# A cubic and a power of two as two bf16 tiles from GpSimd, multiplied on VectorE, in a fused SSM and attention kernel

## The chip, the cores and the metric

The kernel runs on one core of one Trainium2 chip. The metric is the device time of one execution in microseconds; the time before is the median of three runs.

## The reference

One input `x` of 2048 rows and 1024 columns (bf16) goes through two branches, and a gate mixes them row by row:

```python
g = sigmoid((x * gate_w).sum(-1, keepdims=True))
# branch A: a diagonal complex state space model, 1024 states
Lam_bar = exp(dt * Lam);  B_bar = ((Lam_bar - 1.0) / Lam)[:, None] * Bmat
Bu = einsum("bld,pd->blp", x, B_bar)
h  = Lam_bar * h + Bu[:, t]              # for t in 0 .. 2047
a  = 2.0 * einsum("blp,dp->bld", hseq, Cmat).real + x * Dskip
# branch B: attention, 32 heads of 32 columns
q, k, v = split(x @ wqkv);  p = softmax(q k^T * 32 ** -0.5);  b = (p v) @ wo
out = g * a + (1 - g) * b
```

## The kernel before

The kernel records operations in an order that it plans by itself, engine by engine, and each engine then runs its list in order, waiting on semaphores where an operation needs another engine's result.

**Bursts.** Attention is cut into 8 groups of four heads, each into 8 units of 256 queries, each into 8 bursts of 256 keys: 512 bursts, and the loop variable `p` of `build` counts them (64 to a group; `pg` is the place in the group). `burst` (L1612) issues the scores on TensorE (L1624, eight matmuls into four banks) and two exps on ScalarE (L1643), each over 1024 columns: `exp(0)`, and later `exp(1)`. `pv` (L1709) multiplies earlier exps with V into bank 6. At the end of a unit `normalize` (L1722, L1723, then a transposing DMA) takes the result out. The score banks form three slots, so the scores of the next burst wait for `exp(0)` of this one.

**Dense work.** The other matmuls run in the gaps, four of 512 columns to a burst, all in bank 7, in chains of eight to twenty: B's product `u` (L1457), projections of Q, K and V for the next group (L1426, L1445), C's product `c` (L1504), and at the end the output projection (L1535). VectorE evacuates bank 7 after each chain (L1461, L1433, L1451, L1517, L1547). VectorE also does the scan of the state space model in `item_ops` (L1353, L1362), from u tiles that go out to memory and come back (`ld_u`, L1474).

**VectorE's exps.** ScalarE is relieved of part of the exps. For bursts that are chosen by `X_PLAN` and `X_AT`, `exp(1)` takes only 768 columns (L1640), and VectorE computes the exp of the last 256. Two such bursts make a pair. `x_in` (L1633) scales the scores to a fixed-point number of 32 bits, whose upper half is the integer part and whose lower half is the fraction of a power of two. `x_ops` then takes three f32 steps on VectorE over the 512 columns of the pair: two steps of a cubic in the fraction (L1667, L1668), and a third that adds the integer part (L1664); GpSimd scales that sum into 16 bits that are read as a bf16 (L1665). `x_pv` (L1688) multiplies them with V, at a fixed burst (`x_when`). `exp(1)` waits for `x_in`.

**The plan of VectorE.** In every burst the planner fills the time until the next evacuation with ready work: first the pair's steps (`xbg`), then scan items (`bg`), then the rest (`bg2`), by costs that are written in the code (0.73 for the steps of a pair, `X_LAST` for the last). `dve_t` is the time at which the plan has VectorE free.

**Weights.** All loads are issued by SP's queue in order. Q's weights have one buffer and are loaded at `pg` 28 for the next group; those of K and V have two buffers and are loaded at `pg` 25, a group earlier. C is loaded (L1081) two tiles in every fourth burst from `C_LOADS` = 28 on. The rows of Wo are loaded into buffers that have come free: two rows at burst 386, four when the last chain of C is done, one shortly after the last projections, and one row into B's place.

Of the kernel before, what the change touches and what calls it, by code (L numbers as in the profile page):

```python
# [6 lines left out]
BF = mybir.dt.bfloat16  # L7
# [3 lines left out]
ALU = mybir.AluOpType  # L11
# [720 lines left out]
class GpPhaseA:  # L732
# [24 lines left out]
    def first(self, name):  # L757
        return self.alias.pop(name, [])
# [164 lines left out]
GROUPS = 8  # L923
# [6 lines left out]
REST = 508  # L930
FIRST = 16
RING = 60
C_LOADS = 28

X_AT = ((0, 2), (4, 6), (0, 4))
X_PLAN = (64, 72, 80, 88, 92, 96, 100, 104, 108, 112, 116, 120, 124, 128, 132, 136, 144, 152, 160, 168, 172, 176, 180, 184, 188, 192, 200, 208, 216, 224, 228, 232, 236, 240, 244, 248, 252, 256, 260, 264, 272, 280, 288, 296, 304, 312, 316, 320, 324, 328, 332, 336, 344, 352, 356, 360, 364, 368, 372, 376, 380, 384, 388, 392, 396, 400, 404, 408, 412, 416, 420, 424, 428, 432, 436, 440, 444, 448, 452, 456, 460, 464, 468, 472, 476, 480, 484, 488, 492, 496, 500, 504)
# [12 lines left out]
class Dense:  # L949
# [9 lines left out]
class FastPath:  # L959

    def __init__(self, nc, S, es, d, flag):
        self.nc, self.S, self.d, self.flag = nc, S, d, flag
        E = es.enter_context
        T = lambda name, shape, dt: E(nc.sbuf_tensor("f_" + name, shape, dt))
# [9 lines left out]
        self.wq = wb[:, 0:1024].rearrange("p (a n) -> p a n", a=8)  # L974
        self.wkv = wb[:, 1024:5120].rearrange("p (s q a n) -> p s q a n", s=2, q=2, a=8)
        self.bT = wb[:, 5120:8192].rearrange("p (s a n) -> p s a n", s=3, a=8)

        row = lambda o, n: wb[:, o:o + 1024 * n].rearrange("p (a n) -> p a n", a=n)
        self.wo3 = [row(1024, 2), row(5120, 3), row(3072, 1), self.cT[0][:, 0:1, :], self.cT[0][:, 1:2, :]]
        self.wo = [(self.wo3[0][:, a, :], "wo0") for a in range(2)] + [(self.wo3[4][:, 0, :], "wo4")] + [(self.wo3[1][:, a, :], "wo1") for a in range(3)]  # L980
        self.wo += [(self.wo3[3][:, 0, :], "wo3"), (self.wo3[2][:, 0, :], "wo2")]
# [5 lines left out]
        self.hpx = wb[:, 5120:8192].rearrange("p (k n) -> p k n", k=6)  # L987
        ub = T("ub", [128, 2, 2, 512], BF)
        self.ub = [ub[:, 0], ub[:, 1]]
        self.tq = T("tq", [128, 2, 512], BF)  # L990
        self.xi = T("xi", [128, 2, 2 * X_COLS], I32)
        self.xq = T("xq", [128, 2 * X_COLS], F32)
        self.xp = T("xp", [128, 2 * X_COLS], BF)
        self.ut = T("ut", [128, 2, 512], F32)
        self.ht = T("ht", [128, 2, 512], BF)
        self.prow = self.ht[0:40, 0, 0:128]
# [66 lines left out]
                     [], [("xr", r + k) for k in range(n // 128)], "ld_x", eng)  # L1063

    def w_of(self, g, part):
        return (self.wkv[:, g % 2, part - 1], ("w", g % 2, part)) if part else (self.wq, ("w", 0, 0))

    def ld_w(self, g, part, eng="sp"):
        cb = 1024 * part + 128 * g
# [583 lines left out]
    def x_ops(self, b):  # L1653

        xi, xq, xp = self.xi[:, b % 2], self.xq, self.xp
        lo = xi.bitcast(mybir.dt.uint16)[:, 0::2]
        hi = xi.bitcast(mybir.dt.int16)[:, 1::2]
        bits = xp.bitcast(mybir.dt.int16)[:]
        w = 65536.0
        i2, p2 = [("xi", b % 2, 0), ("xi", b % 2, 1)], [("xp", 0), ("xp", 1)]  # L1660

        def last():
            assert self.x_out == len(self.x_done)
            self.dve(lambda e: e.scalar_tensor_tensor(xq[:], hi, 128.0 / X_K, xq[:], ALU.mult, ALU.add), i2 + ["xq"], ["xq"], "x_q")  # L1664
            self.pool(lambda e: e.tensor_scalar(bits, xq[:], X_K, 128.0 * (E0 + 126.0), ALU.mult, ALU.add), ["xq"], p2, "x_p")  # L1665
            self.x_done.add(b)
        return [(0.73, 0.0, lambda: self.dve(lambda e: e.scalar_tensor_tensor(xq[:], lo, E2 / E3 * w, lo, ALU.add, ALU.mult), i2, ["xq"], "x_q")),  # L1667
                (0.73, 0.0, lambda: self.dve(lambda e: e.scalar_tensor_tensor(xq[:], xq[:], E1 / E3 * w * w, lo, ALU.add, ALU.mult), ["xq"] + i2, ["xq"], "x_q")),  # L1668
                (X_LAST, 0.0, last)]

    def x_flush(self):
        c, wait, f = self.xbg.pop(0)
        f()
        self.dve_t += c

    def x_pv(self, b):

# [56 lines left out]
    def build(self):  # L1734
# [7 lines left out]
        self.begin()  # L1742
        for m in range(3):
            self.ld_b(m)
        for part in (1, 2):
            self.ld_w(1, part)
        self.plan()
        self.pt_own = {}
        self.x_of, self.x_batch, self.x_when = {}, [], {}
        self.xbg, self.x_done, self.x_out = [], set(), 0  # L1750
        self.opening()

        S.tok_w["O"] = S.tok_w[("bank", 6)]
# [25 lines left out]
        outs, k = [], 0  # L1779
# [2 lines left out]
            k += kind != "rest"  # L1782
        cur = None
        first = FIRST
        wo1 = wo6 = last = False
        nal = nc = 0
        self.c_end = 0
        log = self.log = []
# [1 line left out]
        for p in range(first, NBURST):  # L1790
# [38 lines left out]
            while self.later and self.later[0][0] <= p:  # L1829
                self.later.pop(0)[1]()  # L1830

            if pg == 25 and g + 2 < GROUPS:
                assert g or not (proj[0] or cur and cur.tag == "proj")
                for part in (1, 2):
                    self.ld_w(g + 2, part)
            if pg == 28 and g + 1 < GROUPS:
                assert not (cur and cur.tag == "proj")
                self.ld_w(g + 1, 0)
            wsv = self.d["B_wo"].rearrange("(a p) n -> p a n", p=128)
            if p == 386:  # L1840
                self.dma(lambda e: e.dma_start(self.wo3[0], wsv[:, 0:2, :]), [], ["wo0"] + [("w", 0, q) for q in (1, 2)], "ld_wo")
            if not cs and cur is None and not wo1 and self.c_left[3] == 0:
                wo1 = True
                self.dma(lambda e: e.dma_start(self.wo3[1], wsv[:, 3:6, :]), [], ["wo1"] + [("bT", r) for r in range(3)] + [("hp", 8, k) for k in range(6)], "ld_wo")
            if g >= 6 and not wo6 and not cs and self.c_left[3] == 0:
                wo6 = True
                self.dma(lambda e: e.dma_start(self.wo3[3], wsv[:, 6:7, :]), [], ["wo3", ("cT", 0, 0), ("cTf", 0, 0, 0), ("cTf", 0, 0, 1)], "ld_wo")
                self.dma(lambda e: e.dma_start(self.wo3[4], wsv[:, 2:3, :]), [], ["wo4", ("cT", 0, 1), ("cTf", 0, 1, 0), ("cTf", 0, 1, 1)], "ld_wo")
            if g >= 6 and not last and not proj[7] and not us and not cs and cur is None and not self.bg:

                last = True
                xs = [("xr", r) for r in range(16)]
                assert wo1 and wo6
                self.dma(lambda e: e.dma_start(self.wo3[2], wsv[:, 7:8, :]), [], ["wo2"] + [("w", 1, q) for q in (1, 2)] + xs, "ld_wo")
# [51 lines left out]
            while self.xbg or self.bg or self.bg2:  # L1906
# [39 lines left out]
                f()  # L1946
                if c > 0:
                    self.dve_t = now + c
            if ended is not None:
                ended.evac()  # L1950
                self.dve_t = max(self.dve_t, dense_end) + 0.65
# [4 lines left out]
    def tail(self):  # L1956
# [41 lines left out]
        for r in range(2):  # L1998
            for cb in range(2):
                bank = 2 + r + 2 * cb  # L2000
                w = dict(acc=[("tb", bank)]) if cb == 0 else dict(writes=[("tb", bank)] + ([("S", 2)] if r == 0 else []), **({} if r == 0 else dict(acc=[("S", 2)])))
                S.op("pe", lambda e, r=r, cb=cb, bank=bank: e.matmul(ps[:, bank, :], OT[:, 7, 1792 + 128 * r:1920 + 128 * r], wo[7][0][:, 512 * cb:512 * (cb + 1)],
                                                                    start=(cb == 1), stop=True), reads=[("OT", 7, 7, r), "wo2"], name="tail", **w)
# [132 lines left out]
```

## Time and profile before

| | before |
|---|---|
| median of three runs | 926.67 us (926.38 to 930.31) |
| profiled execution | 928.11 us |
| its span in the profile | 926.3 us, mean granted TensorE clock 0.996 |
| PE, ACT, DVE, POOL busy | 97%, 98%, 82%, 9% |
| mean share of the DMA engines, by queue 1 | 36.3% |

PE is TensorE's matmuls, PEld its weight loads, ACT is ScalarE, DVE VectorE, POOL GpSimd, SP the queue that issues the DMAs. A row of the groups ends with busy time, the mean duration of one in ns, and the idle time of the engine before them with what ended it. Durations of consecutive instructions overlap, so the pace of an engine is read from starts. A row of the timeline gives the start, the length in us, the engine, the line, and how many instructions are merged; idle time before it and what ended it stand in brackets. A row of the windows gives the stretch, its length, and each engine's busy time with its instructions.

### The profile page before, as it was taken

What the parts mean: (1) busy time and instruction counts of PE and PEld (TensorE: products, weight loads), DVE (VectorE), ACT (ScalarE), POOL (GpSimd) and SP (SyncE); (2) the same over time, 40 slices, a digit from 0 to 9 for tenths busy, and PEclk for the clock granted to TensorE, in tenths of its full rate; (3) what the DMA queues carried; (4) which work ended last, traced back from release to release, by engine and by line L of the source; (5) the groups of instructions that cost most, each with busy time, mean ns of one, the idle gap of its engine ahead of it and who ended that gap; (6) DMA issues with size and microseconds to landing.
All of it is one profiled execution on the core that took longest, in us unless ns stands there. A gap on an engine that the chain in (4) does not pass through costs nothing.

```text
span 926.3 us, 33979 instructions
## 1 busy us (share of the span) xinstructions
PE 902.5 (97%) x15316; PEld 503.9 (54%) x15316; DVE 758.4 (82%) x1310; ACT 907.3 (98%) x1034; POOL 86.8 (9%) x156
## 2 busy tenths in 40 slices
PE   8899999999999999999999999999999999999996
PEld 4554754557555565546655565555655655445553
DVE  2788989998989999989989999899988655776665
ACT  6999999999999999999999999999999999999996
POOL 2000000111000101011111020000010010001010
PEclk9999999999999999999999999999999999999998
DMA  9569747750457101272012511413001112424312
GB/s 195 87 116 184 93 84 138 144 116 5 81 113 152 50 20 49 67 147 53 19 51 65 126 45 31 104 63 103 20 15 43 31 51 77 156 83 128 114 62 75
DMA packets 170934, 77.69 MB, mean 84 GB/s; under 512 B 147232, under 2 KB 155424, under 8 KB 170784
## 3 DMA queue, kind: packets, MB, share of 16 engines
q1 hardware_dynamic: 168624, 74.94, 36.3%
q8 instruction: 121, 1.98, 0.9%
q10 hardware_dynamic: 2160, 0.53, 0.3%
q14 instruction: 29, 0.24, 0.1%
HBM read 25.18 MB, written 20.97 MB: 50 GB/s over the span
## 4 chain that ended last, share of the span: by engine, by line
PE 52%; ACT 40%; DVE 4%; DMA 2%; SPq 1%; issue 1%; POOL 0%; DVEq 0%; ACTq 0%
ACT f_pt L1643 32%; PE f_ps L1709 14%; PE f_ps L1624 10%; PE f_ps L1426 9%; PE f_ps L1504 7%; PE f_ps L1457 6%; ACT f_pt L1640 5%; PE f_ps L1445 5%; SPq L1062 1%; ACT f_cT L1643 1%; PE f_ps L1688 1%; DMA f_xT<-in_A_x_dram 1%; ACT f_Et L1643 1%; DMA f_wb<-in_A_B_im_dram 1%; DMA f_ub<-u_scratch 0%
## 5 line engine op out<-in xcount | busy, mean ns | idle before, releaser
L1643 ACT ACTIVATE f_pt<-f_ps 128x1024 bf16<-128x1024 f32 x760 | 728.8, 1090 | 1.5 <-PE f_ps L1624 1.3
L1709 PEld LDWEIGHTS f_ps<-f_V,f_pt 128*128 128x128 bf16 x7184 | 222.2, 96 | 95.3 <-issue 68.7
L1709 PE MATMUL f_ps<-f_V,f_pt 128*128 128x33 bf16 x7184 | 258.0, 178 | 0.0
L1624 PE MATMUL f_ps<-f_Q,f_K 32*128 32x256 bf16 x4096 | 203.3, 273 | 10.8 <-ACT f_pt L1643 3.3
L1640 ACT ACTIVATE f_pt<-f_ps 128x768 bf16<-128x768 f32 x184 | 165.3, 898 | 0.7 <-PE f_ps L1624 0.6
L1624 PEld LDWEIGHTS f_ps<-f_Q,f_K 32*128 32x128 bf16 x4096 | 60.7, 92 | 148.0 <-ACT f_pt L1643 120.6
L1457 PE MATMUL f_ps<-f_xT,f_wb 128*128 128x512 bf16 x512 | 131.5, 379 | 1.6 <-DMA f_wb<-in_A_B_im_dram 0.7
L1665 POOL TENSOR_SCALAR f_xp<-f_xq 128x512 int16<-128x512 f32 x92 | 67.3, 732 | 646.0 <-DVE f_xq L1664 471.3
L1426 PE MATMUL f_ps<-f_xT,f_wb 128*128 128x512 bf16 x464 | 119.3, 379 | 0.1
L1633 DVE TENSOR_SCALAR f_xi<-f_ps 128x256 int32<-128x256 f32 x184 | 77.4, 421 | 17.6 <-PE f_ps L1624 13.3
L1362 DVE TENSOR_TENSOR_SCAN f_ht<-f_pf,f_init,f_ut 128x512 bf16<-128x512 f32 x64 | 81.3, 1279 | 0.0
L1504 PE MATMUL f_ps<-f_cT,f_hp 128*128 128x512 bf16 x272 | 74.5, 379 | 0.1
L1667 DVE SCALAR_TENSOR_TENSOR f_xq<-f_xi 128x512 f32<-128x512 uint16 x92 | 63.7, 692 | 3.2
L1668 DVE SCALAR_TENSOR_TENSOR f_xq<-f_xq,f_xi 128x512 f32<-128x512 f32 x92 | 63.6, 692 | 3.1
L1664 DVE SCALAR_TENSOR_TENSOR f_xq<-f_xi,f_xq 128x512 f32<-128x512 int16 x92 | 63.5, 690 | 2.6
L1457 PEld LDWEIGHTS f_ps<-f_xT,f_wb 128*128 128x128 bf16 x512 | 40.1, 96 | 40.5 <-issue 8.6
L1535 PE MATMUL f_ps<-f_wb,f_OT 128*128 128x512 bf16 x188 | 61.2, 381 | 0.4 <-DVE f_Et L1547 0.4
L1445 PE MATMUL f_ps<-f_wb,f_xT 128*128 128x128 bf16 x896 | 59.3, 219 | 0.0
L1426 PEld LDWEIGHTS f_ps<-f_xT,f_wb 128*128 128x128 bf16 x464 | 36.1, 96 | 35.6 <-issue 7.6
L1461 DVE CAST f_ub<-f_ps 128x512 bf16<-128x512 f32 x64 | 44.1, 688 | 10.4 <-PE f_ps L1457 9.7
L1445 PEld LDWEIGHTS f_ps<-f_wb,f_xT 128*128 128x128 bf16 x896 | 50.4, 97 | 3.8 <-issue 3.8
L1722 DVE RECIPROCAL f_rc<-f_ps 128x8 f32<-128x8 f32 x63 | 13.1, 207 | 47.6 <-PE f_ps L1688 43.5
(149 smaller groups left out, 822.5 us busy)
## 6 DMA issues: line engine op xcount, KB each, us to landing
u_scratch<-f_ub SPq DMA_DIRECT2D x64, 128.0 KB, 2.1
f_ub<-u_scratch SPq DMA_DIRECT2D x32, 256.0 KB, 3.0
ag_scratch<-f_Ag SPq DMA_DIRECT2D x32, 256.0 KB, 2.0
f_hp<-ag_scratch SPq DMA_DIRECT2D x32, 256.0 KB, 3.0
f_wb<-in_B_wqkv_dram SPq DMA_DIRECT2D x21, 256.0 KB, 4.1
out_dram<-f_xT SPq DMA_DIRECT2D x16, 256.0 KB, 2.2
f_OT<-f_On SPq DMA_TRANSPOSE x63, 2.3
f_wb<-in_B_wo_dram SPq DMA_DIRECT2D x1, 768.0 KB
```

Source lines behind the costliest of these rows:

```text
L1362: ops.append((1.24, lambda ri=ri: dve(lambda e: e.tensor_tensor_scan(ht[:, ri, :], rr, ut[:, ri, :], self.init[:, ri, j:j + 1], ALU.mult, ...
L1426: mms.append((1, lambda e, f, l, a=a, w=w: e.matmul(ps[:, bank, :], w[:, a, :], xT[:, a, 512 * ch:512 * (ch + 1)], start=f, stop=l), [tok] ...
L1445: m = e.matmul(ps[:, bank, 128 * q:128 * (q + 1)], xT[:, a, 128 * kt:128 * (kt + 1)], w[:, a, :], start=(a == 0), stop=(a == 7))
L1457: mms.append((1, lambda e, f, l, a=a: e.matmul(ps[:, 7, :], bT[:, (2 * n + ri) % 3, a, :], xT[:, a, 512 * ch:512 * (ch + 1)], start=f, sto ...
L1504: mms.append((1, lambda e, f, l, j=j, ri=ri, h=h: e.matmul(ps[:, 7, :], h[:, cols], cT[ri][:, j, 512 * cb:512 * (cb + 1)], start=f, stop=l ...
L1624: m = e.matmul(ps[:, 2 * sl[h // 2] + h % 2, 256 * kl:256 * (kl + 1)], K[32 * h:32 * h + 32, g % 2, 128 * kt:128 * (kt + 1)], Q[32 * h:32 ...
L1633: first = self.dve(lambda e: e.tensor_scalar(self.xi[:, b % 2, X_COLS * n:X_COLS * (n + 1)], ps[:, 2 * s + 1, 512 - X_COLS:512], X_A, X_LO ...
L1640: self.S.op("act", lambda e: e.activation(flat(self.tile[p]), flat(ps[:, 2 * s:2 * s + 2, :]), ACT.Exp, scale=SCALE), reads=[("S", s)], wr ...
L1643: self.act(lambda e: e.activation(self.tile[p], ps[:, 2 * s:2 * s + 2, :], ACT.Exp, scale=SCALE), [("S", s)], [("pt", p)], "exp")
L1665: self.pool(lambda e: e.tensor_scalar(bits, xq[:], X_K, 128.0 * (E0 + 126.0), ALU.mult, ALU.add), ["xq"], p2, "x_p")
L1667: return [(0.73, 0.0, lambda: self.dve(lambda e: e.scalar_tensor_tensor(xq[:], lo, E2 / E3 * w, lo, ALU.add, ALU.mult), i2, ["xq"], "x_q") ...
L1709: m = e.matmul(ps[:, 6, o:o + 33], self.tile[p][:, h2, 256 * kl + 128 * qt:256 * kl + 128 * (qt + 1)], V[:, g % 2, 2 * i + kl, h, :], star ...
```

## The change

The third f32 step is taken out. While VectorE takes the first step, GpSimd turns the integer part into the bits of a power of two, a bf16 tile (`xe`); after the second step GpSimd scales the sum and adds the constant, which completes the cubic as a second bf16 tile (`xm`); VectorE multiplies the two tiles. The planner's cost of that last step is 0.36, and it is not planned sooner than 0.9 after the second step (`X_GAP`). `X_PLAN` holds 96 pairs in place of 92, at other bursts.

The two new tiles take the room of a second buffer: the weights of Q, K and V now have one buffer each. K's and V's are loaded at `pg` 0 (group 1's K at burst 17), Q's at 38, and the projections of K start no sooner than `pg` 4, those of Q no sooner than 42. C's loads start at burst 32. Seven of the eight rows of Wo are loaded one by one after the last chain of C, into C's and B's places, the eighth after the last projections.

```diff
-C_LOADS = 28
+C_LOADS = 32
+W_AT = (38, 0, 17)
-X_PLAN = (64, 72, 80, 88, 92, ... 92 places)
+X_PLAN = (64, 72, 80, 88, 96, ... 96 places)
-X_LAST = 0.735
+X_LAST = 0.36
-X_K = 128.0 * E3 / 65536.0 ** 3
+X_K = E3 / 65536.0 ** 3
+X_GAP = 0.9
...
-        wb = T("wb", [128, 8192], BF)
+        wb = T("wb", [128, 6144], BF)
+        self.wqkv = [wb[:, 1024 * k:1024 * (k + 1)].rearrange("p (a n) -> p a n", a=8) for k in range(3)]
...
+        self.xm = T("xm", [128, 2 * X_COLS], BF)
+        self.xe = T("xe", [128, 2 * X_COLS], BF)
...
-        bits = xp.bitcast(mybir.dt.int16)[:]
+        bits = self.xe.bitcast(mybir.dt.int16)[:]
+        def first():
+            self.dve(lambda e: e.scalar_tensor_tensor(xq[:], lo, E2 / E3 * w, lo, ALU.add, ALU.mult), i2, ["xq"], "x_q")
+            self.pool(lambda e: e.tensor_scalar(bits, hi, 128.0, 128.0 * 127.0, ALU.mult, ALU.add), i2, ["xe"], "x_e")
+        def second():
+            self.dve(lambda e: e.scalar_tensor_tensor(xq[:], xq[:], E1 / E3 * w * w, lo, ALU.add, ALU.mult), ["xq"] + i2, ["xq"], "x_q")
+            self.pool(lambda e: e.tensor_scalar(self.xm[:], xq[:], X_K, E0, ALU.mult, ALU.add), ["xq"], ["xm"], "x_m")
         def last():
-            self.dve(lambda e: e.scalar_tensor_tensor(xq[:], hi, 128.0 / X_K, xq[:], ALU.mult, ALU.add), i2 + ["xq"], ["xq"], "x_q")
-            self.pool(lambda e: e.tensor_scalar(bits, xq[:], X_K, 128.0 * (E0 + 126.0), ALU.mult, ALU.add), ["xq"], p2, "x_p")
+            self.dve(lambda e: e.tensor_tensor(xp[:], self.xm[:], self.xe[:], ALU.mult), ["xm", "xe"], p2, "x_p")
...
-                proj[g][8 + c].after = max(16 * c, 32)
+                proj[g][c].after = W_AT[1] + 4
+                proj[g][8 + c].after = max(16 * c, W_AT[0] + 4)
...
-            if pg == 25 and g + 2 < GROUPS:
-                for part in (1, 2):
-                    self.ld_w(g + 2, part)
-            if pg == 28 and g + 1 < GROUPS:
+            if pg == W_AT[1 if g else 2] and g + 1 < GROUPS:
+                self.ld_w(g + 1, 1)
+                if g:
+                    self.ld_w(g + 1, 2)
+            if pg == W_AT[0] and g + 1 < GROUPS:
                 self.ld_w(g + 1, 0)
...
-                    if c == X_LAST and self.x_out != len(self.x_done):
+                    if c == X_LAST and (xs or now < self.x_ready or self.x_out != len(self.x_done)):
                         break
```

More of the change, by code (lines that the diff above doesn't have):

```diff
@@ L1784, in build @@
         first = FIRST
-        wo1 = wo6 = last = False
+        wo1 = last = False
         nal = nc = 0
@@ L1838, in build @@
+            if pg == W_AT[0] and g + 1 < GROUPS:
+                assert not proj[0]
                 self.ld_w(g + 1, 0)
             wsv = self.d["B_wo"].rearrange("(a p) n -> p a n", p=128)
-            if p == 386:
-                self.dma(lambda e: e.dma_start(self.wo3[0], wsv[:, 0:2, :]), [], ["wo0"] + [("w", 0, q) for q in (1, 2)], "ld_wo")
-            if not cs and cur is None and not wo1 and self.c_left[3] == 0:
+            if not wo1 and not cs and cur is None and self.c_left[3] == 0:
@@ L1843, in build @@
                 wo1 = True
[L1844 to L1848, printed above, removed]
+                for a in range(7):
+                    j = a if a < 3 else a - 3
+                    x = [("cT", 0, j), ("cTf", 0, j, 0), ("cTf", 0, j, 1)]
+                    if a in (3, 4, 5):
+                        x = [("bT", a - 3)] + [("hp", 8, k) for k in (2 * a - 6, 2 * a - 5)]
+                    self.dma(lambda e, a=a: e.dma_start(self.wo[a][0], wsv[:, a, :]), [], ["wo%d" % a] + x, "ld_wo")
@@ L1849, in build @@
             if g >= 6 and not last and not proj[7] and not us and not cs and cur is None and not self.bg:
                 last = True
[L1852 to L1854 removed]
+                assert wo1
+                self.dma(lambda e: e.dma_start(self.wo[7][0], wsv[:, 7, :]), [], ["wo7", ("cT", 0, 4), ("cTf", 0, 4, 0), ("cTf", 0, 4, 1)], "ld_wo")
@@ L2002, in tail @@
                 S.op("pe", lambda e, r=r, cb=cb, bank=bank: e.matmul(ps[:, bank, :], OT[:, 7, 1792 + 128 * r:1920 + 128 * r], wo[7][0][:, 512 * cb:512 * (cb + 1)],
-                                                                    start=(cb == 1), stop=True), reads=[("OT", 7, 7, r), "wo2"], name="tail", **w)
+                                                                    start=(cb == 1), stop=True), reads=[("OT", 7, 7, r), "wo7"], name="tail", **w)
             if r == 0:
```

30 lines of the change are left out of this document (13 added, 17 removed).

## The prediction

> **What bounds the kernel now.** I read the page's busy shares, then the groups by line, then the waits, then stages, then single stretches of the timeline.
>
> ```profile
> span 926.3 us, 33979 instructions
> PE 902.5 (97%) x15316; PEld 503.9 (54%) x15316; DVE 758.4 (82%) x1310; ACT 907.3 (98%) x1034; POOL 86.8 (9%) x156
> L1643 ACT ACTIVATE f_pt<-f_ps 128x1024 bf16<-128x1024 f32 x760 | 728.8, 1090 | 1.5 <-PE f_ps L1624 1.3
> L1640 ACT ACTIVATE f_pt<-f_ps 128x768 bf16<-128x768 f32 x184 | 165.3, 898 | 0.7 <-PE f_ps L1624 0.6
> PEld f_ps L1624 <- ACT f_pt L1643: 120.6, 312, 1.0
> 600.00:720.00 120.00, 119.94 (x2090) 69.61 (x2089) 107.79 (x178) 119.99 (x139) 10.02 (x15) 1.00 0.17 48
> ```
>
> ScalarE is busy for 98% of the span, and for 119.99 of 120 us in the stage from 600 to 720 (columns: PE, PEld, DVE, ACT, POOL). TensorE's weight loads for the scores wait for its exps 312 times. So the kernel is a train of exps, two per burst, with TensorE a hair behind; VectorE has 12.2 us of slack in that stage. Only two things save time: exp columns taken off ScalarE, and stalls that break the train.
>
> The profiled execution took 928.11 us for a span of 926.3, so 1.8 us lie outside. The median of the three runs is 926.67, 1.44 below it. I sum against 928.11 and take 1.44 off.
>
> **Four more pairs.** The plan goes from 92 to 96 pairs (six more in bursts 256 to 319, two fewer in 64 to 127): eight more bursts whose second exp has 768 columns.
>
> ```profile
> 702.03 2.89 ACT L1643 ACTIVATE f_pt<-f_ps 128x1024 bf16<-128x1024 f32 x3
> 704.74 0.89 ACT L1640 ACTIVATE f_pt<-f_ps 128x768 bf16<-128x768 f32 x1
> 705.43 2.94 ACT L1643 ACTIVATE f_pt<-f_ps 128x1024 bf16<-128x1024 f32 x3
> 708.15 0.93 ACT L1640 ACTIVATE f_pt<-f_ps 128x768 bf16<-128x768 f32 x1
> 708.88 2.95 ACT L1643 ACTIVATE f_pt<-f_ps 128x1024 bf16<-128x1024 f32 x3
> ```
>
> Durations overlap, so I read starts: three full exps from 702.03 to 704.74 are 0.90 each; a short one holds the next back by 0.69 (704.74 to 705.43) or 0.73 (708.15 to 708.88). Saving 0.17 to 0.21 per burst, and I take 0.17, since TensorE is the later one in the slower case: 8 x 0.17 = **-1.4 us** (bounds 0, if TensorE takes it all, and -1.7).
>
> **Q's weights and C's loads later.** Before, at burst 28, SP issues two transposes of C, Q's weights, and only then the u tile that VectorE's scan item needs.
>
> ```profile
> 65.46 1.29 SPq L1081 DMA_TRANSPOSE f_cT<-in_A_C_re_dram  x1
> 66.79 1.30 SPq L1081 DMA_TRANSPOSE f_cT<-in_A_C_im_dram  x1
> 68.14 1.28 SPq L1071 DMA_DIRECT2D f_wb<-in_B_wqkv_dram  x1
> 69.53 0.67 SPq L1474 DMA_DIRECT2D f_ub<-u_scratch  x1
> 73.34 0.69 DVE L1353 TENSOR_TENSOR f_ht<-f_ub,f_Et 128x1024 bf16<-128x1024 bf16 x1 [2.39 <-DMA f_ub<-u_scratch]
> 75.27 0.57 PE L1709 MATMUL f_ps<-f_V,f_OT 128*128 128x33 bf16 x16 [1.24 <-DVE f_On L1723]
> 77.36 1.94 ACT L1643 ACTIVATE f_OT<-f_ps 128x1024 bf16<-128x1024 f32 x2 [1.34 <-PE f_ps L1624]
> ```
>
> This is a chain: 3.9 us of issues ahead of the u load, VectorE idle 2.39, the normalization behind it late, TensorE idle 1.24, ScalarE idle 1.34. In the changed program's order C starts at burst 32 and Q's weights load at 38, so at burst 28 the u load stands alone. Moved up 3.9 us, it is earlier than VectorE's wait of 2.39 needs: **-1.3 us**. What is late next: at burst 32 C's first pair stands ahead of the next u load in both programs, and that wait doesn't show before. Bounds: 0, if the jam reappears at 36 to 38, where no u load is queued until 43, and -1.3.
>
> The other weight loads leave the bursts 25 and 28 of each group for 0 and 38. Two stalls hang on what surrounds them and on late products:
>
> ```profile
> 408.60 2.04 ACT L1643 ACTIVATE f_pt<-f_ps 128x1024 bf16<-128x1024 f32 x2
> 409.55 1.04 PE L1457 MATMUL f_ps<-f_xT,f_wb 128*128 128x512 bf16 x4 [0.69 <-DMA f_wb<-in_A_B_im_dram]
> 410.97 1.02 ACT L1643 ACTIVATE f_pt<-f_ps 128x1024 bf16<-128x1024 f32 x1 [0.33 <-PE f_ps L1624]
> 470.29 0.27 PE L1688 MATMUL f_ps<-f_V,f_xp 128*128 128x33 bf16 x4 [0.27 <-POOL f_xp L1665]
> ```
>
> At 409 a transposed B tile is late; by the program's order three weight loads stand on the queue in the five bursts before it. Two exps take 2.37 instead of 1.81, a loss of 0.56. In the changed order that stretch of u work has no weight load in it. At 470 TensorE waits for the old power-of-two step on GpSimd; the new last step is on VectorE, right behind an x_in, a burst ahead of its use. I take **-0.5 us** for both (bounds 0 and -1). Against it stand new tight places:
>
> ```profile
> f_wb<-in_B_wqkv_dram SPq DMA_DIRECT2D x21, 256.0 KB, 4.1
> ```
>
> Group 7's K weights are now issued at burst 384 for use at 388, and at 434 seven separate Wo loads stand ahead of Ag's loads where three stood. Four bursts are 7 us (702.03 to 705.43 is two), against 4.1 us to land, and the Wo rows are used from burst 444: hidden, up to +1 if the queue is slow. The single buffers of K's and V's weights cost nothing: their last reader is a group back.
>
> **The arithmetic of a pair.**
>
> ```profile
> L1665 POOL TENSOR_SCALAR f_xp<-f_xq 128x512 int16<-128x512 f32 x92 | 67.3, 732 | 646.0 <-DVE f_xq L1664 471.3 <-PE f_ps L1688 161.3 <-PE f_ps L1624 7.2
> L1353 DVE TENSOR_TENSOR f_hp<-f_ut,f_tq 128x512 bf16<-128x512 bf16 x17 | 7.1, 417 | 0.0
> L1664 DVE SCALAR_TENSOR_TENSOR f_xq<-f_xi,f_xq 128x512 f32<-128x512 int16 x92 | 63.5, 690 | 2.6
> L1633 DVE TENSOR_SCALAR f_xi<-f_ps 128x256 int32<-128x256 f32 x184 | 77.4, 421 | 17.6 <-PE f_ps L1624 13.3
> 704.28 0.69 DVE L1667 SCALAR_TENSOR_TENSOR f_xq<-f_xi 128x512 f32<-128x512 uint16 x1
> 705.00 0.69 DVE L1668 SCALAR_TENSOR_TENSOR f_xq<-f_xq,f_xi 128x512 f32<-128x512 f32 x1
> 705.73 0.69 DVE L1664 SCALAR_TENSOR_TENSOR f_xq<-f_xi,f_xq 128x512 f32<-128x512 int16 x1
> 491.37 6.52 ACT L1643 ACTIVATE f_pt<-f_ps 128x1024 bf16<-128x1024 f32 x7
> 491.53 0.69 DVE L1664 SCALAR_TENSOR_TENSOR f_xq<-f_xi,f_xq 128x512 f32<-128x512 int16 x1
> 492.14 0.69 DVE L1353 TENSOR_TENSOR f_ht<-f_ub,f_Et 128x1024 bf16<-128x1024 bf16 x1
> 492.31 0.99 POOL L1665 TENSOR_SCALAR f_xp<-f_xq 128x512 int16<-128x512 f32 x1 [4.99 <-DVE f_xq L1664]
> 492.74 1.10 DVE L1353 TENSOR_TENSOR f_tq<-f_ub,f_Et 128x1024 bf16<-128x1024 bf16 x1
> 699.39 0.62 POOL L1665 TENSOR_SCALAR f_xp<-f_xq 128x512 int16<-128x512 f32 x1 [5.66 <-DVE f_xq L1664]
> ```
>
> The third f32 step cost 0.69, 0.72 from start to start; the product of two bf16 tiles has the shape of the 417 ns group. On paper VectorE saves 0.3 per pair, and as it is off the path, that is worth nothing beyond the four pairs it makes room for. But GpSimd now has two instructions per pair, and the rows at 492 show a collision: its step takes 0.62 alone and 0.99 beside a VectorE instruction with two SBUF inputs, which holds its 0.69; GpSimd ends 0.47 behind that (492.83 to 493.30), and the next such instruction takes 1.10 for 0.69, ending 0.54 behind GpSimd.
>
> In the changed program the power of two is released by the same x_in as the first f32 step, and VectorE's second step follows the first directly in 95 of 96 pairs. VectorE starts its next instruction first in those rows (492.14 against 492.31), so the first step runs clear, GpSimd ends 0.47 behind it and the second step 0.54 behind that: 1.01 instead of 0.72, **0.29 late per pair, 28 us in all**. Behind the cubic step on GpSimd, 18 pairs have two background instructions with SBUF inputs; the second loses 0.41: 7 us. The product waits for GpSimd only in the nine pairs where nothing but background work lies between (some 0.5 each).
>
> Is this on the path? What is queued behind the late step is the evacuation of the dense bank, an x_in, or background work. At 492 the 0.41 hit no exp: seven from 491.37 in 6.52 us are six times 0.90 and a last one. In the stage from 600 to 720 VectorE idles 12.2 us for 15 pairs, 0.81 per pair against 0.29. So I take **+1.0 us**, 3% of 35; bounds 0 and +35. The price of GpSimd's new steps is that of the 0.62 row, the nearest; their inputs are as wide or narrower.
>
> The Trainium skill weighs in on this (SBUF — State Buffer, Who interferes with whom): VectorE and GpSimd share a port pair as an exclusive lock, a VectorE instruction with two SBUF inputs contends with a GpSimd instruction that reads SBUF, and the later one "fully blocks" for the whole instruction. The trace agrees on who collides; of the 0.62 instruction it shows 0.41 lost. By the rule's whole instruction the second step would lose up to 0.62 per pair, 60 us of VectorE's time instead of 28. That feeds the slower rival below.
>
> **Sum.** -1.4 - 1.3 - 0.5 + 1.0 = -2.2: the profiled execution would take 925.9, the median **924.5 us**.
>
> **Rivals.** *The gains are eaten*: TensorE is at 97%, so short exps may just wait for scores, and moved loads may jam elsewhere (group 7's K, the Wo rows). Against it: the short exps quoted, on both sides of dense matmuls, save 0.17 and more. It gives 925.5 to 929, middle 927.
>
> *The lock reaches the path (slower)*: in 50 of 96 pairs background work stands between the late second step and the next evacuation, so that evacuation starts late, the next dense chain waits for the bank, and the scores behind it come late. If these 50 pass on their whole 0.29, that is +14.5, with the gains of 3.2 a net +11.3: 938. It decides where VectorE's idle time per pair falls below 0.29; for it speak the eighteen 0.41s in the same places, against it the 0.81 and the unbroken row at 491.37.
>
> *VectorE's lighter pair speeds up ScalarE's train (faster)*: if all 192 short exps went at 0.69 instead of 0.73, that is 7.7 more, 915.8. TensorE, not VectorE, comes late there, so I give it little.
>
> **How the numbers follow.** Forecast 0.61, gains eaten 0.22, lock on the path 0.11, faster 0.06. A change of 0.5% (4.6 us) is about what a measurement of this kernel can tell from none: below 922.0 lie the faster rival and a little of the forecast's tail, 0.08; above 931.3 the lock, 0.11; between, 0.81. The forecast's own range is 922.5 (all gains, no cost) to 926.5; the eaten gains take it to 929, and a lock that passes on a fifth of its 35 us (+7 - 3.2) to 931: 922.4 to 931.
>
> **What would show it.** Right: POOL busy about 200 us (86.8 - 67.3 + 96 x 1.9), the power of two near 1.1 us (it ends 0.47 behind a first step of 0.69), the cubic 0.62 to 1.0 and the second f32 step near 0.98; VectorE busy 772 to 779, not less (758.4 - 63.5 + 96 x 0.417 + four pairs of two x_in at 0.42 and two steps at 0.69, 8.9, + 28 or 35); no idle of 1.34 on ScalarE near 77 us; the matmuls of L1688 never waiting for the product. Wrong: waits of TensorE for evacuations or of ScalarE for x_in that grow to microseconds; a wait of TensorE on weights; a second step at 0.69.

## The result: 0.6% slower, above the forecast's range

| | before | after |
|---|---|---|
| median of six runs each, same chip | 926.55 us (926.09 to 930.31) | 933.27 us (932.62 to 933.81) |
| ratio to before, 95% interval | | 1.0059 (1.0046 to 1.0073) |
| profiled execution, its span | 928.11, 926.3 us | 932.88, 931.1 us |

The forecast was 924.5 us with a range up to 931.0. The time lies outside it, on the side of the rival in which the lock reaches the path.

The head of the page of after and its two groups of exps, as shown of before:

```profile
span 931.1 us, 33812 instructions
PE 881.0 (95%) x15095; PEld 504.7 (54%) x15316; DVE 763.8 (82%) x1330; ACT 909.2 (98%) x1034; POOL 217.4 (23%) x256
L1646 ACT ACTIVATE f_pt<-f_ps 128x1024 bf16<-128x1024 f32 x752 | 719.3, 1070 | 6.5 <-PE f_ps L1627 5.6
L1643 ACT ACTIVATE f_pt<-f_ps 128x768 bf16<-128x768 f32 x192 | 167.2, 871 | 0.8 <-DVE f_xi L1636 0.5
```

The eight short exps arrived (192, from 184), and still the idle time ahead of the full ones grew from 1.5 to 6.5 us. (PE's 881.0 us must not be read against before's 902.5: 221 matmul records are missing here, 15095 against 15316. The first matmul of every chain of `u`, Q, K and C is among them, the one that waits for bank 7. The same number is missing in e5 and e7 to e10 below, none in e1 to e4. ScalarE's records are whole in all of them.)

The groups of a pair's arithmetic, in the order in which they run:

```profile
L1666 DVE SCALAR_TENSOR_TENSOR f_xq<-f_xi 128x512 f32<-128x512 uint16 x96 | 66.4, 692 | 3.3
L1667 POOL TENSOR_SCALAR f_xe<-f_xi 128x512 int16<-128x512 int16 x96 | 107.4, 1119 | 470.4 <-DVE f_xi L1636 470.4
L1670 DVE SCALAR_TENSOR_TENSOR f_xq<-f_xq,f_xi 128x512 f32<-128x512 f32 x96 | 93.8, 977 | 3.2
L1671 POOL TENSOR_SCALAR f_xm<-f_xq 128x512 bf16<-128x512 f32 x96 | 88.7, 924 | 60.2 <-DVE f_xq L1670 60.2
L1675 DVE TENSOR_TENSOR f_xp<-f_xm,f_xe 128x512 bf16<-128x512 bf16 x96 | 39.7, 413 | 2.2 <-POOL f_xm L1671 2.2
```

The first step runs clear at 692 ns; the power of two on GpSimd takes 1119; VectorE's second step, which alone takes 692 like the first (e2 below), takes 977: 0.285 us late in each pair. The cubic's last step on GpSimd takes 924 on average, where 44 of the 96 take 0.62, so it collides as well, in some of the pairs.

What became of that, in the waits of after:

```profile
ACT f_pt L1646 <- PE f_ps L1627: 5.6, 19, 0.6
PE f_ps L1507 <- DVE f_Ag L1520: 3.8, 7, 0.9
PE f_ps L1429 <- DVE f_Q L1436: 2.5, 5, 0.8
DVE f_xp L1675 <- POOL f_xm L1671: 2.2, 5, 0.4
```

The columns are total us, count and the longest. TensorE's dense matmuls (C at L1507, Q at L1429) now wait for VectorE's evacuations of bank 7, and ScalarE waits 19 times for scores. In before that same wait of ScalarE is 1.3 us, as the group of its exps quoted there shows. For `u` (L1460) this trace names an x_in or a product as what was waited for, but each of these waits stands right behind an evacuation of `u` whose next chain lacks the record of its first matmul. The trace of e4 (below), which is slower than before as well and has all its matmul records, names the evacuation:

```profile
ACT f_pt L1646 <- PE f_ps L1627: 7.1, 20, 1.5
PE f_ps L1460 <- DVE f_ub L1464: 2.6, 8, 0.6
```

The sizes of TensorE's waits in after are a little too large for the same reason, by some 0.2 us for each missing matmul.

One such place in the timeline of after, engine by engine:

```profile
454.04 0.69 DVE L1666 SCALAR_TENSOR_TENSOR f_xq<-f_xi 128x512 f32<-128x512 uint16 x1
454.77 0.98 DVE L1670 SCALAR_TENSOR_TENSOR f_xq<-f_xq,f_xi 128x512 f32<-128x512 f32 x1
455.67 0.68 DVE L1356 TENSOR_TENSOR f_tq<-f_ub,f_Et 128x1024 bf16<-128x1024 bf16 x1
456.38 0.98 DVE L1356 TENSOR_TENSOR f_ut<-f_ht,f_tq 128x512 f32<-128x512 bf16 x1
457.29 0.68 DVE L1436 CAST f_Q<-f_ps 128x512 bf16<-128x512 f32 x1
454.09 1.12 POOL L1667 TENSOR_SCALAR f_xe<-f_xi 128x512 int16<-128x512 int16 x1 [4.02 <-DVE f_xi L1636]
455.83 0.99 POOL L1671 TENSOR_SCALAR f_xm<-f_xq 128x512 bf16<-128x512 f32 x1 [0.62 <-DVE f_xq L1670]
458.02 0.55 PEld L1429 LDWEIGHTS f_ps<-f_xT,f_wb 128*128 128x128 bf16 x4 [0.66 <-DVE f_Q L1436]
458.25 0.81 PE L1429 MATMUL f_ps<-f_xT,f_wb 128*128 128x512 bf16 x3 [0.79 <-DVE f_Q L1436]
459.44 1.02 ACT L1646 ACTIVATE f_pt<-f_ps 128x1024 bf16<-128x1024 f32 x1 [0.30 <-PE f_ps L1627]
```

The second step loses 0.29 to GpSimd's first step, and the second background operation behind it another 0.30 to GpSimd's second. The evacuation of Q stands behind both on VectorE's list and so starts 0.6 us late: 1.10 us behind the last matmul of its chain, where the same evacuation in e7, without GpSimd's steps, starts 0.52 behind it. TensorE's next matmul in order needs that bank, and it idles some 0.6 (the trace has four weight loads but three matmuls here, so the 0.79 includes the missing one); the scores come late, and ScalarE idles 0.30. VectorE's own list has no gap here, so nothing in the stretch takes the delay back.

The windows show two stages: the one from 600 to 720 us, on which the prediction rested, and the one behind it. First after, then a kernel (e7 below) in which GpSimd has neither step:

```profile
600.00:720.00 120.00, 115.99 (x2014) 67.54 (x2043) 109.61 (x185) 118.63 (x136) 33.26 (x30) 1.00 0.17 47
720.00:840.00 120.00, 115.58 (x1987) 65.34 (x2015) 76.75 (x142) 119.04 (x138) 29.92 (x34) 1.00 0.26 82
```

```profile
600.00:720.00 120.00, 118.24 (x2100) 70.67 (x2119) 106.72 (x186) 119.99 (x139) 0.00 (x0) 1.00 0.16 43
720.00:840.00 120.00, 115.65 (x1946) 62.95 (x1978) 69.93 (x143) 119.28 (x138) 0.00 (x0) 1.00 0.30 92
```

From 600 to 720 ScalarE gets 136 exps done where before and e7 get 139, some 2.7 us lost, although VectorE idles for 10.4 of the 120 us. From 720 on, where VectorE has little background work, all three do 138. The starts of the exps tell the same over the whole kernel: at burst 96 after is level with e7, which has the same plan; at 192, 256, 320 and 416 it is 2.5, 4.8, 6.3 and 9.3 us behind; and from 416 to the end it loses nothing more, although the second step of all 23 pairs there still takes 0.98. The evacuations in that last part start 0.07 us behind their last matmul on average in after and 0.06 in e7: the delay is there, but the evacuations are not late for it.

### The profile page after: what moved, and what is told of

Its sections match the earlier page's. It is cut to its first block, busy times and chain, and to the rows that moved or that the text cites. A ratio compares the mean times of both kernels' runs of the same rounds, so it can differ in the third digit from the quotient of the medians.

```text
span 931.1 us, 33812 instructions
## 1 busy us (share of the span) xinstructions
PE 881.0 (95%) x15095; PEld 504.7 (54%) x15316; DVE 763.8 (82%) x1330; ACT 909.2 (98%) x1034; POOL 217.4 (23%) x256
## 4 chain that ended last, share of the span: by engine, by line
PE 49%; ACT 27%; DVE 18%; issue 4%; DMA 1%; POOL 0%; DVEq 0%; SPq 0%; ACTq 0%
ACT f_pt L1646 21%; PE f_ps L1718 12%; PE f_ps L1627 10%; PE f_ps L1507 8%; PE f_ps L1429 7%; PE f_ps L1460 6%; PE f_ps L1448 5%; ACT f_pt L1643 4%; DVE f_xi L1636 3%; DVE f_xq L1666 2%; DVE f_xq L1670 2%; DVE f_ht L1365 2%; DVE f_ut L1356 2%; DVE f_Ag L1520 1%; ACT f_cT L1646 1%
## 5 line engine op out<-in xcount | busy, mean ns | idle before, releaser
L1646 ACT ACTIVATE f_pt<-f_ps 128x1024 bf16<-128x1024 f32 x752 | 719.3, 1070 | 6.5 <-PE f_ps L1627 5.6
L1667 POOL TENSOR_SCALAR f_xe<-f_xi 128x512 int16<-128x512 int16 x96 | 107.4, 1119 | 470.4 <-DVE f_xi L1636 470.4
L1643 ACT ACTIVATE f_pt<-f_ps 128x768 bf16<-128x768 f32 x192 | 167.2, 871 | 0.8 <-DVE f_xi L1636 0.5
L1460 PE MATMUL f_ps<-f_xT,f_wb 128*128 128x512 bf16 x448 | 117.7, 379 | 10.8 <-DVE f_xi L1636 3.1
L1429 PE MATMUL f_ps<-f_xT,f_wb 128*128 128x512 bf16 x406 | 106.8, 379 | 9.4 <-DVE f_Q L1436 2.5
L1671 POOL TENSOR_SCALAR f_xm<-f_xq 128x512 bf16<-128x512 f32 x96 | 88.7, 924 | 60.2 <-DVE f_xq L1670 60.2
L1670 DVE SCALAR_TENSOR_TENSOR f_xq<-f_xq,f_xi 128x512 f32<-128x512 f32 x96 | 93.8, 977 | 3.2
L1636 DVE TENSOR_SCALAR f_xi<-f_ps 128x256 int32<-128x256 f32 x192 | 80.5, 419 | 18.2 <-PE f_ps L1627 14.0
L1365 DVE TENSOR_TENSOR_SCAN f_ht<-f_pf,f_init,f_ut 128x512 bf16<-128x512 f32 x64 | 80.9, 1273 | 0.0
L1507 PE MATMUL f_ps<-f_cT,f_hp 128*128 128x512 bf16 x240 | 67.6, 379 | 5.5 <-DVE f_Ag L1520 3.4
L1666 DVE SCALAR_TENSOR_TENSOR f_xq<-f_xi 128x512 f32<-128x512 uint16 x96 | 66.4, 692 | 3.3
L1460 PEld LDWEIGHTS f_ps<-f_xT,f_wb 128*128 128x128 bf16 x512 | 40.1, 96 | 42.5 <-issue 10.9
L1429 PEld LDWEIGHTS f_ps<-f_xT,f_wb 128*128 128x128 bf16 x464 | 36.1, 96 | 40.0 <-issue 7.6
L1368 POOL CAST f_hl<-f_ht 128x2 f32<-128x2 bf16 x24 | 11.1, 461 | 156.4 <-DVE f_ht L1365 156.2
```

The lines of the kernel that those rows point to most:

```text
L1365: ops.append((1.24, lambda ri=ri: dve(lambda e: e.tensor_tensor_scan(ht[:, ri, :], rr, ut[:, ri, :], self.init[:, ri, j:j + 1], ALU.mult, ...
L1429: mms.append((1, lambda e, f, l, a=a, w=w: e.matmul(ps[:, bank, :], w[:, a, :], xT[:, a, 512 * ch:512 * (ch + 1)], start=f, stop=l), [tok] ...
L1460: mms.append((1, lambda e, f, l, a=a: e.matmul(ps[:, 7, :], bT[:, (2 * n + ri) % 3, a, :], xT[:, a, 512 * ch:512 * (ch + 1)], start=f, sto ...
L1507: mms.append((1, lambda e, f, l, j=j, ri=ri, h=h: e.matmul(ps[:, 7, :], h[:, cols], cT[ri][:, j, 512 * cb:512 * (cb + 1)], start=f, stop=l ...
L1636: first = self.dve(lambda e: e.tensor_scalar(self.xi[:, b % 2, X_COLS * n:X_COLS * (n + 1)], ps[:, 2 * s + 1, 512 - X_COLS:512], X_A, X_LO ...
L1643: self.S.op("act", lambda e: e.activation(flat(self.tile[p]), flat(ps[:, 2 * s:2 * s + 2, :]), ACT.Exp, scale=SCALE), reads=[("S", s)], wr ...
```

## The experiments

Ratios are to the kernel before on the same chip, each timed in five rounds. Its median was 926.55 us on the chip of after and 928.57 to 930.0 on the others, though its fastest execution was 926.0 to 926.7 on every chip: a stall of varying length sits in it (see e3). So a difference between after and a run on another chip is given twice, by the ratios and by the spans of the two traces.

| run | ratio | 95% interval |
|---|---|---|
| after | 1.0059 | 1.0046 to 1.0073 |
| e2: after, no power-of-two step on GpSimd | 0.9973 | 0.9956 to 0.9990 |
| e7: after, neither step on GpSimd | 0.9945 | 0.9923 to 0.9967 |
| e3: before, loads moved alone | 0.9968 | 0.9951 to 0.9986 |
| e4: after, before's 92 pairs | 1.0042 | 1.0026 to 1.0059 |
| e1: e4, second step planned at 0.98 | 0.9982 | 0.9966 to 0.9997 |
| e5: after, GpSimd's first step issued behind its second | 0.9984 | 0.9969 to 1.0000 |
| e8: before, 342 ns on VectorE behind each second step | 1.0094 | 1.0067 to 1.0121 |
| e9: the same with 183 ns | 1.0042 | 1.0022 to 1.0062 |
| e10: e8 in every fourth pair only | 1.0031 | 1.0016 to 1.0046 |

The theory: the lock between VectorE and GpSimd makes the second step 0.29 late, the plan does not know it, and evacuations, then TensorE, then ScalarE come late. The rivals: more short exps or the moved weights cost the time; the longer chain of a pair is late for its use; VectorE's delay is harmless and something else on GpSimd's side costs.

### e2: the power of two taken off GpSimd

```diff
-            self.pool(lambda e: e.tensor_scalar(bits, hi, 128.0, 128.0 * 127.0, ALU.mult, ALU.add), i2, ["xe"], "x_e")
...
+        pool(lambda e: e.memset(self.xe[:], 1.0), [], ["xe"])
```

The power of two is left out here: its tile holds ones.

> The changed kernel without GpSimd's power-of-two step per pair: the tile is set to ones once at the start, so the exps of the 256 columns lack their power of two; everything else, and the order on every other engine, is as changed. Theory A (the port lock makes VectorE's second step 0.29 late, which the plan doesn't know; evacuations come late and TensorE and ScalarE with them): the second step falls from 0.98 to 0.69, and the time falls from 1.0059 of before to 0.997 to 1.000 (924 to 926.5). Rival B (the lock is harmless; twelve more short bursts between bursts 150 and 330 overload TensorE, or weights with one buffer come late): the second step falls as well, but the time stays at 1.004 to 1.007 (930.5 to 933).

Measured 0.9973. The group of the second step, and the chain of work that ended last, in shares of the span:

```profile
L1670 DVE SCALAR_TENSOR_TENSOR f_xq<-f_xq,f_xi 128x512 f32<-128x512 f32 x96 | 66.4, 692 | 3.2
PE 60%; ACT 30%; DVE 5%; SPq 1%; DMA 1%; issue 1%; POOL 0%; DVEq 0%; ACTq 0%
```

In after that chain holds VectorE for 18% of the span:

```profile
PE 49%; ACT 27%; DVE 18%; issue 4%; DMA 1%; POOL 0%; DVEq 0%; SPq 0%; ACTq 0%
```

With the GpSimd step gone, the second step takes 692 ns again, VectorE's share of the chain falls to 5%, and 0.0086 of the time is back, some 8 us (6.6 by the spans, 931.1 and 924.5). Part of the 18% may be due to after's missing records; e4, which is slower than before too and has none missing, stands at 13%. All that the change lost against before hangs on that one instruction per pair, which no wait of VectorE in after's trace names.

### e3: the moved loads alone

```diff
-C_LOADS = 28
+C_LOADS = 32
...
-                proj[g][8 + c].after = max(16 * c, 32)
+                proj[g][8 + c].after = max(16 * c, 42)
...
-            if pg == 28 and g + 1 < GROUPS:
+            if pg == 38 and g + 1 < GROUPS:
```

> The kernel before with three numbers of the change alone: C's loads from burst 32, Q's weights at 38 of each group, Q's projections no sooner than 42. Both theories: the idle time of 1.34 us on ScalarE near 77 us goes, and the time falls by 1 to 2.5 us, to 0.9973 to 0.999 (924.2 to 925.7). If it stays at 1.000, the jam only moved, and that term of the sum was wrong.

Measured 0.9968, some 3.0 us. ScalarE in after, in the stretch where before idled 1.34 us:

```profile
73.31 1.94 ACT L1646 ACTIVATE f_pt<-f_ps 128x1024 bf16<-128x1024 f32 x2
75.21 1.94 ACT L1646 ACTIVATE f_OT<-f_ps 128x1024 bf16<-128x1024 f32 x2
77.03 1.95 ACT L1646 ACTIVATE f_Et<-f_ps 128x1024 bf16<-128x1024 f32 x2
```

No idle time is left here, and e3's trace has none there either. The wait of 0.69 for a B tile at 409 is gone, and the largest for such a tile is 0.2 in e3 and in after. So two of the stalls that the prediction named are gone in these traces (e4, with after's loads, has one B tile 1.6 late, at 142); the interval reaches from 1.3 to 4.6 us, which the 1.3 + 0.5 of the prediction lies inside.

That it is more than 1.8 has a reason which one trace of before can't show: the stall near 77 us varies. e8, e9 and e10 have before's loads and its order up to the first pair, at burst 64, and ScalarE's longest idle time in that place is 2.19, 3.87 and 2.25 in their traces, where before's had 1.34. In e9:

```profile
80.07 1.94 ACT L1644 ACTIVATE f_OT<-f_ps 128x1024 bf16<-128x1024 f32 x2 [3.87 <-PE f_ps L1625]
```

It fits that before's executions lie between 926.0 and 933.4 us, and those of each kernel with the moved loads within 1.2 to 3.5 us of each other. e3 has the lowest ratio of the versions that compute the whole, though the intervals of e1 and e5 overlap its own.

### e4 and e1: fewer pairs, and a plan that knows

e4 is after with `X_PLAN` of before, its 92 places. e1 changes one line more:

```diff
-        return [(0.73, 0.0, first), (0.73, 0.0, second), (X_LAST, 0.0, last)]
+        return [(0.73, 0.0, first), (0.98, 0.0, second), (X_LAST, 0.0, last)]
```

> The changed kernel with the old list of 92 pairs. Theory A: the lock still makes each second step 0.29 late and the plan still fills the time that isn't there, so most of the loss stays: 1.003 to 1.006 (929.5 to 932). Rival B: without the extra short bursts between 150 and 330 the loss goes, and the earlier loads stay: 0.997 to 0.9995 (924 to 926).

> The changed kernel with the old list of 92 pairs, and the second step planned at 0.98 instead of 0.73, which is what it takes in the trace. Theory A: the second step still takes 0.98, but evacuations no longer come late (their mean delay behind the last matmul falls from 0.20 to about 0.10 us), and the time falls to 0.997 to 1.000 (924 to 926.5), below the run with 92 pairs and the old cost by 4 us or more. Rival B: as that run, within 1 us.

Measured 1.0042 and 0.9982. With before's pairs the loss stays, so the four more pairs and their short exps are not its cause; the intervals of e4 and after overlap, and whether the four pairs bring or cost anything is not told by them. With one number of the plan raised by 0.25, the loss of 0.0060 is gone. The groups of the second step in e4 and in e1:

```profile
L1670 DVE SCALAR_TENSOR_TENSOR f_xq<-f_xq,f_xi 128x512 f32<-128x512 f32 x92 | 89.8, 977 | 3.1
```

```profile
L1670 DVE SCALAR_TENSOR_TENSOR f_xq<-f_xq,f_xi 128x512 f32<-128x512 f32 x92 | 80.9, 879 | 2.1
```

The step still takes 879 ns on average in e1, so some two thirds of the lock is paid there, and it costs little, since less is planned behind it: on the same chip e1's median is 1.0 us above that of e3, which has before's pairs and arithmetic and no such lock. Part of the gain is another one: with the higher cost the plan puts the second step directly behind the first in only 61 of 92 pairs, and the others are less disturbed.

### e5: GpSimd's first step moved behind its second

```diff
-X_GAP = 0.9
+X_GAP = 1.5
...
-            self.pool(lambda e: e.tensor_scalar(bits, hi, 128.0, 128.0 * 127.0, ALU.mult, ALU.add), i2, ["xe"], "x_e")
...
             self.pool(lambda e: e.tensor_scalar(self.xm[:], xq[:], X_K, E0, ALU.mult, ALU.add), ["xq"], ["xm"], "x_m")
+            self.pool(lambda e: e.tensor_scalar(bits, hi, 128.0, 128.0 * 127.0, ALU.mult, ALU.add), i2 + ["xq"], ["xe"], "x_e")
```

> The changed kernel with GpSimd's power of two behind the cubic, released by the second step instead of x_in, and the product planned no sooner than 1.5 behind that step instead of 0.9. Theory A: the second step is clear again (0.69), so 0.29 per pair is gone; but both GpSimd steps now run beside what follows the second step, so where background work with two SBUF inputs follows (50 of 96 pairs) it collides there, up to two times 0.41 per pair. Net the time falls to about 0.998 to 1.002. Rival C (what costs is only where the 0.29 stands, ahead of the pair's own second step, not VectorE's lateness as such): 0.996 to 0.998, as without the power of two.

Measured 0.9984: better than after by 0.0075 (5.9 us by the spans, 931.1 and 925.2), at the low end of what the theory gave; the interval reaches into the range of rival C as well, so this run alone doesn't part them. The groups:

```profile
L1669 DVE SCALAR_TENSOR_TENSOR f_xq<-f_xq,f_xi 128x512 f32<-128x512 f32 x96 | 66.4, 692 | 3.2
L1671 POOL TENSOR_SCALAR f_xe<-f_xi 128x512 int16<-128x512 int16 x96 | 63.6, 663 | 7.6
L1670 POOL TENSOR_SCALAR f_xm<-f_xq 128x512 bf16<-128x512 f32 x96 | 90.0, 938 | 569.0 <-DVE f_xq L1669 569.0
```

The same work on the same engines, released by the second step instead of the x_in: the second step is clear, and the power of two takes 663 ns on average (0.62 us in 77 of the 96) instead of 1119. The cubic's step at 938 still collides. The product now waits for the power of two 21 times, 6.9 us in all, a longer chain per pair than in after, in a faster kernel: a late product isn't what costs.

### e7: neither step on GpSimd

The edit of e2, and with it:

```diff
-            self.pool(lambda e: e.tensor_scalar(self.xm[:], xq[:], X_K, E0, ALU.mult, ALU.add), ["xq"], ["xm"], "x_m")
...
+        pool(lambda e: e.memset(self.xm[:], 1.0), [], ["xm"])
```

> The changed kernel with neither of GpSimd's two steps per pair: both bf16 tiles are set to ones once at the start, so the exps of the 256 columns are left out; VectorE's two steps and its product stay. Theory A: against the run without the power of two alone (0.9973) the 18 collisions behind the cubic step and the product's waits go, some 7 us of VectorE's time; at the price seen so far (9 us of kernel time for about 28 of VectorE's) that is 1 to 2.5 us: 0.995 to 0.997. If the cubic's collisions are hidden: 0.997 to 0.998.

Measured 0.9945, 5.1 us under before. So the pairs, the loads and the lighter arithmetic were worth 5.1 us, and GpSimd's two steps cost 1.0059 - 0.9945 = 0.0114, some 10.6 us (8 to 13, from the two intervals): 8.0 for the power of two, 2.6 for the cubic. The spans of the traces give 9.0 (931.1 and 922.1), 6.6 and 2.4. The VectorE time behind it is 33.8 us in after's trace: 27.4 in the second steps (96 x 0.285) and 6.4 in 18 instructions that collide with the cubic's step. So 27 to 31% of it arrives.

### e8, e9, e10: a delay without GpSimd

Nothing of the change is in these. VectorE gets one instruction behind the second step whose result nobody reads, and which the plan doesn't count. e9 has 24 columns in place of 176; e10 has the 176 under a condition, so that only every fourth pair (b % 4 == 0) gets it.

```diff
+        self.dly = T("dly", [128, 176], BF)
...
+            self.dve(lambda e: e.scalar_tensor_tensor(self.dly[:], xq[:, 0:176], 1.0, xq[:, 0:176], ALU.add, ALU.mult), ["xq"], ["dly"], "dly")
```

> The kernel before with one more VectorE instruction behind each second step, 176 columns in f32 from one tile into a spare one, some 0.3 us, which the plan of VectorE doesn't count; GpSimd and loads as before. Theory A (any unplanned 0.3 us per pair makes evacuations late): 1.004 to 1.009, as the lock does it. Rival D (it is the lock's own doing, for example GpSimd's steps or the tiles coming late, and plain VectorE time is covered by its 18% idle): 0.999 to 1.002.

> The kernel before with an unplanned VectorE instruction of 24 columns (not 176) behind the second step of each of 92 pairs: by the earlier delay run's 342 ns for 176 columns and 692 for 512, some 0.18 us of duration, about 0.15 of delay, half the dose. It asks whether a delay costs in proportion to its size or only past a threshold. In proportion (a third of it arrives, as with 0.31): 92 x 0.15 / 3 = 4.6 us, 1.004 to 1.006. Threshold (the slack behind a pair swallows what is small): below 1.002.

> The same 176 columns (342 ns) behind the second step, but only in every fourth pair (23 of 92). It asks whether single late steps, with three undisturbed pairs between them, cost as much each as a train of them. My prediction's reading (an isolated delay hits no exp, the plan's idle time takes it back): 1.000, within 0.0008. In proportion (a third of 23 x 0.31): 2.4 us, 1.002 to 1.0035. Not additive, each late step costs only because the one before it left no room: below 1.001 as well, with the dose of all 92 at 1.0094.

Measured 1.0094, 1.0042 and 1.0031. The groups of the added instruction, in that order:

```profile
L1665 DVE SCALAR_TENSOR_TENSOR f_dly<-f_xq 128x176 bf16<-128x176 f32 x92 | 31.5, 342 | 3.1
```

```profile
L1665 DVE SCALAR_TENSOR_TENSOR f_dly<-f_xq 128x24 bf16<-128x24 f32 x92 | 16.8, 183 | 3.1
```

```profile
L1666 DVE SCALAR_TENSOR_TENSOR f_dly<-f_xq 128x176 bf16<-128x176 f32 x23 | 7.9, 342 | 0.8
```

The expectations reckoned with delays of 0.31 and 0.15 us. The starts of VectorE's instructions show more, here in one pair of e8:

```profile
456.98 0.69 DVE L1664 SCALAR_TENSOR_TENSOR f_xq<-f_xq,f_xi 128x512 f32<-128x512 f32 x1
457.70 0.34 DVE L1665 SCALAR_TENSOR_TENSOR f_dly<-f_xq 128x176 bf16<-128x176 f32 x1
458.08 0.69 DVE L1669 SCALAR_TENSOR_TENSOR f_xq<-f_xi,f_xq 128x512 f32<-128x512 int16 x1
```

From the start of the second step to that of the third it is 1.10 us in e8, 0.94 in e9 and 0.72 to 0.73 in before. So the delays are 0.38, 0.22 and 0.38 us, and their sums 34.6, 20.0 and 8.6 us; what arrives by the ratios is 8.7, 3.9 and 2.9 us, so 25, 20 and 33% (the intervals leave 18 to 33, 10 to 29 and 17 to 50). No threshold below which the delay is swallowed shows, down to 0.22 us. Whether a late step needs a late neighbour to cost is told less surely than e10's ratio looks: in its trace the first exp of burst 64 is already 2.6 us behind before's, from the stall near 77 us, ahead of any pair, and from there to the last burst it falls back by 1.5 us, 17% of its dose. e8 and e9 fall back by 8.8 and 4.5 us in that stretch, 25 and 23%. So lone late steps do cost, perhaps less each.

A bare VectorE delay of 34.6 us costs 8.7 us; the 33.8 us that GpSimd brings cost 9.0 to 10.6. So no other effect of GpSimd is needed. e8's waits show the same pattern as after's, ScalarE for scores and TensorE for the evacuations of C and of `u`:

```profile
ACT f_pt L1644 <- PE f_ps L1625: 5.0, 17, 0.6
PE f_ps L1505 <- DVE f_Ag L1518: 4.1, 9, 0.6
PE f_ps L1458 <- DVE f_ub L1462: 2.4, 5, 0.6
```

## Why the prediction was wrong, step by step

**The step that failed** is "Is this on the path?". The collision itself was right: 0.29 per pair was forecast and 0.285 measured, a second step "near 0.98" is 0.977, a power of two "near 1.1 us" is 1.119, POOL "about 200 us" is 217.4. The 35 us of VectorE delay were then taken at 3%, +1.0 us. They measure 33.8 and cost 9.0 us by the spans and 10.6 by the ratios, 27 to 31%.

Two readings led there. The first was one row: at 492 a loss of 0.41 hit no exp. It was one collision, with scan items behind it. e10 shows that lone delays cost 0.07 (its trace) to 0.13 us (its ratio) each on average; a single one that costs nothing is no contradiction to that, and I made it the rule. The second was an average: 0.81 us of idle time per pair in the stage from 600 to 720, against 0.29. In that same stage after loses three exps with 10.4 us of idle time on VectorE. Idle time takes a delay back only if it lies between the late step and the next evacuation. The planner fills exactly that stretch with background work, up to the time at which it expects the bank, so the idle time lies behind the evacuation instead. I measured this in the traces for the chains of bursts 64 to 443, as the start of an evacuation less the end of its last matmul: on average 0.10 us in before and e3, 0.20 in after, 0.18 in e4, 0.12 in e2, 0.14 in e5, 0.09 in e1 and e7, 0.25, 0.17 and 0.13 in e8, e9 and e10; the kernels stand in nearly the order of their times.

The prediction had the right mechanism among its rivals, with 50 of 96 pairs named for it, but let it begin only "where VectorE's idle time per pair falls below 0.29" and gave it 0.11. That condition is what was wrong: the rival needed no shortage of idle time. Its price, 14.5 us if all 50 pairs pass on all of it, was the right order for 9.0 to 10.6.

**Four more pairs, -1.4; loads, -1.3; stalls, -0.5.** Together -3.2; e7 puts the gains at 5.1 us, with an interval of 3.1 to 7.2. e3 gives the loads 3.0 us where 1.8 was forecast, since the stall that they remove is often longer than in the one trace that was read. The starts of the exps in e7's trace, against before's, part the gains of those two executions: 1.4 us come between bursts 32 and 36 (the stall near 77), 0.6 between 192 and 224 (the B tile at 409), 2.6 between 256 and 320, where six more pairs stand, and 0.7 are lost between 64 and 128, where there are two fewer. So the four pairs are worth some 1.9 us here, a little over the bound of 1.7, together with whatever before's own collisions cost in those bursts; a gain of the lighter arithmetic elsewhere doesn't show. At 470 in before the matmuls waited for the product; in after those of L1697 never wait for it, as forecast.

**The product** was forecast to wait in nine pairs for some 0.5 each; it waits five times, 2.2 us in all, as the row above shows.

**VectorE's busy time** was forecast at 772 to 779 and is 763.8. The steps themselves have the forecast durations. Before's own collisions, 14 of some 0.3 us, fell away with the old step and were not taken out of the sum; that is 4.7 us of the gap. The rest is overlap, which busy time counts once: consecutive instructions of VectorE overlap by 52.6 us in after, by 44.7 in before.

**The rule of the Trainium skill** (SBUF — State Buffer, Who interferes with whom) that the instruction which comes second fully blocks while the first holds the ports was weighed with up to 0.62 per pair. The trace shows 0.285 for the second step, near the 0.29 worked out from the rows at 492. The block isn't quite full: in the rows at 454 the second step ends 0.54 us behind GpSimd's, where alone it takes 0.69. The rule was right on who collides and on the direction.

**What stays open.** Why a fifth to a third arrives, and not more or less, is not derived: it comes out of where evacuations stand behind pairs in this plan, and another plan would have another share. Before has collisions of its own, 14 of 0.23 to 0.42 us with its one GpSimd step; what they cost was not tried apart. The differences between after and the runs on other chips carry the varying stall in before; a kernel without it, timed on every chip, would have been the better base.

## What to carry to other kernels

In a hand-planned order a delay that the plan does not count is not covered by the engine's idle time elsewhere: measure the share that arrives (here about a quarter, from 0.22 us up), or write the delay into the plan's cost, which here brought it to some 1 us. Before one engine's work is given to another, ask which instructions will run beside it, not only whether it is free: GpSimd was idle 91% of the time and VectorE never waited for its power of two, yet it cost 7 to 8 us. And don't take an average of idle time, nor a single undisturbed row, for the cover of a term that is 28 us long; look at each place where the next wait stands behind the late step. And if a stall depends on when loads land, read it in several traces before its size goes into a sum.

## What the runs showed of the hardware

Instructions of VectorE with two SBUF inputs and of GpSimd stretched each other here, but not by their whole length: 692 becomes 977 ns on VectorE, 0.62 us becomes 1.12 on GpSimd. Beside the scan (L1365), which takes 1.27 us, the cubic's step takes 1.52 instead of 0.62 (17 pairs of after). The point at which GpSimd's step was released decided who paid: with the power of two behind the cubic's step (e5) it takes 663 ns on average and the second step 692, for the same work. A short unplanned delay is enough to show: one instruction of 183 ns, 24 columns wide, in each pair moved the whole kernel by 0.42% (0.22 to 0.62).
